# A second level of seven products for one unit of a fused attention and MLP kernel

## The chip, the cores and the metric

The kernel runs on one core of one Trainium2 chip. The metric is the device time of one execution in microseconds (us). The kernel before was run three times: median 203.09 us, from 202.88 to 203.41. Besides, one execution was taken with the hardware profiler; it took 203.15 us, and its trace spans 201.3 us from the first to the last instruction. TensorE had its full clock all the time.

## The reference

```
B, H, S, Ns, D = 8, 8, 512, 32, 64;  d_model, d_ff = 512, 2048
a     = softmax(x @ state^T / sqrt(D))            # per batch and head
xread = a @ state                                 # 512 rows of a batch
sread = softmax(state @ x^T / sqrt(D)) @ x        # 32 rows of a batch
h     = concat([xread, sread]) as (B * 544, 512)  # heads side by side
out   = gelu(h @ w_in) @ w_out                    # w_in 512 x 2048, w_out 2048 x 512
```

Inputs and output are fp32. The kernel computes its products in bf16 and sums them in fp32.

## The kernel before, in words

**Stages.** The eight batches b = 0 to 7 are done one after the other. For the 512 token rows of a batch, `state` and `w_in` are first multiplied (`p_mm`, L435), which gives P (256 x 2048, in two halves t); it is copied out of PSUM by ScalarE (ACT) and VectorE (DVE). The attention weights of a batch are made one batch ahead: `scores` (L325), `norm` (L347) on DVE, a transpose by DMA (`atr_dma`). A block `M` (`mm1`, L501) is two matmuls of 128x128 by 512 columns and a Gelu on ACT; 16 blocks make the hidden rows g of a batch (128 x 16 x 512).

**The second product by seven.** The product g @ w_out of batches 1 to 7 isn't done by eight quarter products but by seven, in the manner of Strassen and Winograd. The contraction (16 chunks of 128), the token rows (256 and 256) and the output columns (256 and 256) are each cut in two. A unit `X(b, name)` (L651) is one of these products: 16 matmuls of 128x128 by 256 columns. Units "1", "2" and "4" read quarters of g as they are; "5", "6", "7" and "3" read sums that `g_sum` (L608) makes on DVE. The differences of w_out for the right operand are made once by `w_diff` (L563). The units collect in four PSUM banks, o0 to o3: bank 0 has "2", bank 1 "1", "6" and "7", bank 2 "5" and "3", bank 3 "4" (`BANK`, L642). Between units of a bank, ACT takes a copy (`snap`, L647: c2, c4, u, s5), and DVE adds bank and copy into the output rows (`add`, L644), which SP sends out. Unit "2" of batch b fills c2; the addition behind unit "1" reads it.

**The read-outs.** The 32 state rows of a batch (sread) are a sum over the batch's tokens: `reads_mm` (L886) does 32 small matmuls per batch with the copy `xo` of x, ACT copies the bank (`sraw`), DVE divides (`reads_norm`, L903), and `srts` (L421) transposes the result into XSR. For all batches together they go through w_in and w_out in batch 7 (`read_out_slot`, `SR`, `R`). `rearr_ones` (L230) makes `xo` on GpSimd (POOL) from batch 2 on, `rearr` (L221) the copy `x4` for the transposes. Each has two buffers, for even and odd batches. `hold_for` (L942) makes the POOL queue wait for a block's Gelu, so that a load behind it is issued no earlier.

**What sets the order.** There is no scheduler: every engine runs its instructions in the order of the code, and waits only for what an instruction needs. For b = 2 to 7 the code goes through eight slot pairs p = 0 to 7, each with the blocks 2p and 2p+1 of the batch. Units "1", "6", "5" and "7" of the batch before follow in p = 0, 1, 2 and 3, unit "3" in p = 5. Also in p = 5, `p_all` (L917) does the reads of this batch and the whole P of the next, with ACT and DVE copies; its tiles take o0, o1, o3 and o2 and four buffers of a second pool with the tag f, which also holds the results of the blocks and the scores. Then come unit "2" (p = 5) and unit "4" (p = 7) of the batch itself. In batches 2 to 5 the read of the batch itself is done in p = 5, in batch 6 those of 6 and 7.

The lines of the profile that belong to these steps: L626 units, L506 blocks, L441 P, L931 its copies, L893 reads, L901 `sraw`, L424 and L429 transposes of the reads, L616 g sums, L645 additions, L649 snaps, L757 and L775 sums for the read-outs, L797 and L863 read-outs, L225 and L235 copies on POOL.

Of the kernel before, what the change touches and what calls it, by code (L numbers as in the profile page):

```python
# [9 lines left out]
FP32 = mybir.dt.float32  # L10
BF16 = mybir.dt.bfloat16
# [6 lines left out]
def kernel(  # L18
# [36 lines left out]
    def otile(shape, name, at=None):  # L55
        if at is None:
            at = turn[0] % 4
            turn[0] += 1
        return ps_o.tile(shape, FP32, name=name, tag=f"o{at}")
# [55 lines left out]
    def load_x(b):  # L115
        xb = xin.tile([128, H, SJ * D], BF16, name="xb", tag="xb")
        nc.gpsimd.dma_start(out=xb, in_=xr[b])
        xbs[b] = xb
# [111 lines left out]
    def rearr_ones(b):  # L230
        A = atts[b]
        eng = nc.vector if b < 2 else nc.gpsimd
        src = xbs[b].rearrange("p (t c) (j d) -> p t c j d", t=2, d=D)
        for t in range(2):
            eng.tensor_copy(  # L235
                out=A.xo[:, :, :, 2 + 64 * t:66 + 64 * t].rearrange("p j c d -> p c j d"),
                in_=src[:, t],
            )
# [222 lines left out]
    def burst(chunks, b_read=None):  # L461
        done = []
        first = len(chunks) < 4 and b_read is not None
        if first:
            sread(b_read)
        for i, (b, f) in enumerate(chunks):
            done.append((b, f, p_mm(b, f, ftile if i < 2 else otile)))
        for x in done[:2]:
            p_copy(*x)
        if b_read is not None and not first:  # L470
            sread(b_read)
        for x in done[2:3]:
            p_copy(*x)
        if b_read is not None:
            sread_out(b_read)
        for x in done[3:]:
            p_copy(*x)
# [66 lines left out]
    def mm2_m(b, m):  # L544
        for j in range(SJ):
            if m == 0:
                ops[b, j] = otile([128, d_model], "op")
            nc.tensor.matmul(  # L548
                ops[b, j],
                lhsT=gs[b][:, m, j * 128:(j + 1) * 128],  # L550
                rhs=w_out_bf[:, m, :],
                start=(m == 0),
                stop=(m == MC - 1),
            )
# [23 lines left out]
    def w_rhs(name):  # L578
        return {"1": b11, "2": b21, "3": b22}.get(name) if name in "123" else w_t[name]

    xs = {}
    left, right = slice(0, NH), slice(NH, d_model)
    G_SUMS = {
# [7 lines left out]
    def g_q(b, h, k):  # L591
        return gs[b][:, MH * k:MH * k + MH, 256 * h:256 * h + 256]
# [15 lines left out]
    def g_sum(b, names, home=None):  # L608
        got = g_lhs.setdefault(b, {})
        for name in names:  # L610
            x, y, op = chain(name, lambda h, k: g_q(b, h, k), got)
            if home is None:
                got[name] = apool.tile([128, MH, 256], BF16, name="gsum", tag="gsum")
            else:
                got[name] = home
            nc.vector.tensor_tensor(out=got[name], in0=x, in1=y, op=op)  # L616
# [18 lines left out]
    def c_tile(name):  # L635
        return cpool.tile([128, 2, NH], FP32, name=name, tag=name)
# [7 lines left out]
    def add(out, x, y):  # L644
        nc.vector.tensor_tensor(out=out, in0=x, in1=y, op=ALU.add)  # L645
# [37 lines left out]

    def c21(b):
        add(xs[b, "o", 1][:, :, left], xs[b, 1], xs[b, "c4"])

    def rows_out(h, js, ns, eng):
        b = B - 1
# [197 lines left out]
    def reads_mm(bs):  # L886
        sr = ftile([128, len(bs), 2, 65], "sr")
        for i, b in enumerate(bs):
            A = atts[b]
            for t in range(2):  # L890
                for j in range(SJ):
                    for c in range(HC):
                        nc.tensor.matmul(  # L893
                            sr[32 * c:32 * c + 32, i, t, :],
                            lhsT=A.e[:, 2 * j + t, 32 * c:32 * c + 32],
                            rhs=A.xo[:, j, c, 1 + 65 * t:66 + 65 * t],
                            start=(j == 0),
                            stop=(j == SJ - 1),
                        )
        raw = cpool.tile([128, len(bs), 130], FP32, name="sraw", tag="sraw")  # L900
        nc.scalar.copy(out=raw, in_=sr.rearrange("q i t d -> q i (t d)"))  # L901
        return raw

    def reads_norm(bs, raw):
        for i, b in enumerate(bs):
            A = atts[b]
            A.srm = att.tile([128, 2, D], BF16, name="srm", tag="srm")
            inv = att.tile([128, 2], FP32, name="inv", tag="inv")
            nc.vector.reciprocal(out=inv, in_=raw[:, i, 0:130:129])
            nc.vector.tensor_tensor(  # L910
                out=A.srm,
                in0=raw[:, i, 1:129].rearrange("q (t d) -> q t d", t=2),
                in1=inv[:, :].to_broadcast((128, 2, D)),
                op=ALU.mult,
            )

    def p_all(nb, bs):  # L917
        raw = reads_mm(bs)
        done = []
        for f, at in enumerate(((0, None), (None, None), (1, 3), (2, None))):  # L920
            it = iter(at)

            def tiles(shape, name):
                i = next(it)
                return ftile(shape, name) if i is None else otile(shape, name, i)

            done.append((nb, f, p_mm(nb, f, tiles)))
        for b, f, ps in done:
            for t in range(2):
                copy = nc.scalar.copy if t == 0 or f == 0 else nc.vector.tensor_copy  # L930
                copy(out=Ps[b][:, t, f * 512:(f + 1) * 512], in_=ps[t])  # L931
        reads_norm(bs, raw)

    def p_copy_s(b, f, ps):
        for t in range(2):
# [153 lines left out]
    atr(1)  # L1089
    mm2_m(0, 9)  # L1090
    burst([(1, 1), (0, 3)])
    mm2_m(0, 10)
    M(16, 17)
    M(12, 13)
# [51 lines left out]
    for b in range(2, B):  # L1146
        nb = b + 1
        for p in range(8):
            k = 16 * b + 2 * p
            if p == 1 and nb < B:  # L1150
                scores(nb, 0)
                scores(nb, 1)
            if p in (2, 3) and nb < B and (b > 2 or p == 2):
                norm(nb, p - 2)
            if p == 3 and nb + 1 < B:
                xtr_dma(nb + 1)
            if p == 5 and nb < B:
                atr_dma(nb)
            if nb == B and p < 5:
                read_out_slot(p)  # L1160
                if p == 4:
                    r_homes()
                    r_sum("56")
                continue
            if b != 2 or p != 3:
                M(k, k + 1)
            if b == 2 and p == 2:
                M(k + 2, k + 3)
            if b == 2 and p == 1:
                w_diff("7")  # L1170
            if p < 5 and nb < B:
                if p == 0:
                    g_sum(b - 1, "56")
                if p == 2:
                    g_sum(b - 1, "7")
                if p == 3:
                    g_sum(b - 1, "3")
                if p < 4:
                    X(b - 1, "1657"[p])
                if b == 2 and p == 2:  # L1180
                    norm(3, 1)
                    for x in [(2, f, p_mm(2, f, ftile)) for f in (2, 3)]:
                        p_copy(*x)
                if p == 1 and b > 2:
                    sr_w("5216"[b - 3])
            if p == 0 and b + 3 < B:
                hold_for(b, 0)
                load_x(4 if b == 2 else b + 3)
            if p == 6 and b == 2:
                hold_for(b, 12)  # L1190
                load_x(5)
            if p == 0 and nb + 1 < B:
                begin(nb + 1)
                rearr(nb + 1)
            if nb == B:
                if p == 5:
                    R("2")
                    r_sum("73")
                    R("4")
                if p == 6:  # L1200
                    R("1")
                    X(b, "2")
                    R("6")
                    R("5")
                if p == 7:
                    X(b, "4")
                continue
            if p == 5:
                X(b - 1, "3")
                reads = (b, nb) if nb == B - 1 else (b,)  # L1210
                p_all(nb, reads)
                if b == 2:
                    rearr_ones(3)
                    rearr_ones(4)
                elif nb + 1 < B:
                    rearr_ones(nb + 1)
                X(b, "2")
            if p == 7:
                srts(reads)
                X(b, "4")  # L1220
    b = B - 1
    g_sum(b, "56")
# [41 lines left out]
```

## Time and profile before

| | |
|---|---|
| runs | 202.88, 203.09, 203.41 us |
| the profiled execution | 203.15 us, its span 201.3 us |
| a batch (67.4 to 88.6, 88.6 to 109.8, 109.8 to 131.0) | 21.2 us |
| in 88.6 to 109.8: busy PE, DVE, ACT, POOL | 21.15, 15.88, 16.76, 5.30 us |
| one unit (L626), 16 matmuls | 1.75 us on the chain |
| one block pair (L506), 4 matmuls | 0.86 us on the chain |

PE is TensorE's matmuls, PEld its weight loads, DVE VectorE, ACT ScalarE, POOL GpSimd, SP SyncE, whose queue issues DMAs. A row of a group has line, engine, operation, output and inputs, shapes and count, then busy us and mean ns of one, then the idle time before them and who ended it. A row of a timeline has start, duration and the instructions merged in it. A row of the chain has start, duration and what the end of the program waited for then. Matmuls overlap: a row of 16 lasts 0.16 us longer than the next matmul waits.

### The profile page before, as it was taken

How to read it: one execution, taken by the hardware profiler on the slowest of the kernel's cores; microseconds unless marked ns; L12 is line 12 of the kernel's file. 1: busy time of each engine (PE TensorE's matmuls, PEld its weight loads, DVE VectorE, ACT ScalarE, POOL GpSimd, SP SyncE). 2: the span in 40 equal slices, each digit the busy share in tenths (PEclk: the TensorE clock that was granted, in tenths of full speed). 3: DMA queues.
4: the chain of work that ended last, by engine and by line, in shares of the span. 5: the costliest groups of instructions: out<-in, count | busy, mean ns of one | idle time of the engine just before them, and what ended most of it. 6: DMA issues, size and time to landing. Idle time of an engine off the chain costs nothing.

```text
span 201.3 us, 4865 instructions
## 1 busy us (share of the span) xinstructions
PE 195.5 (97%) x2035; PEld 134.6 (67%) x2035; DVE 140.9 (70%) x235; ACT 142.8 (71%) x260; POOL 49.8 (25%) x63
## 2 busy tenths in 40 slices
PE   7899999999999999999999999999999999999994
PEld 2533544465767677676776687677776888878893
DVE  2873774789988569856795678467936787960863
ACT  3684677699896789668967797598948678774220
POOL 8973404423409444040503400120000000000000
PEclk9999999999999999999999999999999999999999
DMA  6999999977594979670696024520128010040054
GB/s 192 188 173 199 206 199 201 188 133 139 90 147 78 227 89 158 133 210 2 71 193 203 9 70 91 147 65 16 37 103 109 3 52 3 4 155 0 7 154 156
DMA packets 40567, 23.16 MB, mean 115 GB/s; under 512 B 21857, under 2 KB 39137, under 8 KB 40545
## 3 DMA queue, kind: packets, MB, share of 16 engines
q0 software_dynamic: 13984, 8.10, 29.9%
q1 hardware_dynamic: 25728, 14.22, 29.3%
q10 hardware_dynamic: 832, 0.52, 0.8%
q8 instruction: 16, 0.26, 0.5%
q14 instruction: 7, 0.05, 0.1%
HBM read 17.30 MB, written 8.91 MB: 130 GB/s over the span
## 4 chain that ended last, share of the span: by engine, by line
PE 91%; DMA 3%; ACT 2%; DVE 1%; issue 1%; SPq 0%; ACTq 0%
PE xp L626 41%; PE hp L506 27%; PE op L548 5%; PE sp L797 3%; PE rp L863 3%; DMA x0f<-in_x_dram 3%; PE op L532 2%; PE xp L704 2%; PE p_ps L441 2%; PE pt L333 2%; ACT P L931 1%; PE sr L893 1%; PE hp L1041 1%; PE aT_ps L374 1%; ACT sraw L901 1%
## 5 line engine op out<-in xcount | busy, mean ns | idle before, releaser
L513 ACT ACTIVATE g<-hp 128x512 bf16<-128x512 f32 x124 | 65.9, 609 | 13.6 <-PE hp L506 13.4
L506 PE MATMUL hp<-AT,P 128*128 128x512 bf16 x248 | 61.0, 379 | 0.0
L626 PEld LDWEIGHTS <-gsum 128*128 128x128 bf16 x416 | 40.5, 98 | 9.4 <-issue 0.4
L626 PE MATMUL xp<-ws,gsum 128*128 128x256 bf16 x320 | 38.2, 273 | 0.0
L506 PEld LDWEIGHTS <-P 128*128 128x128 bf16 x248 | 23.4, 98 | 21.1 <-ACT P L452 0.7
L626 PEld LDWEIGHTS <-g 128*128 128x128 bf16 x336 | 32.5, 98 | 7.1 <-issue 1.6
L626 PE MATMUL xp<-w_out_bf,g 128*128 128x256 bf16 x224 | 26.7, 272 | 0.3
L235 POOL COPY xo<-xb 128x1024 bf16<-128x1024 bf16 x12 | 13.2, 1129 | 36.4 <-PE sr L893 36.4
L616 DVE TENSOR_TENSOR gsum<-g 128x2048 bf16<-128x2048 bf16 x14 | 17.1, 1221 | 5.1 <-ACT g L513 4.5
L225 POOL COPY x<-xb 128x1024 bf16<-128x1024 bf16 x12 | 12.5, 1069 | 18.2 <-DMA xb<-in_x_dram 18.2
L649 ACT COPY c<-xp 128x512 f32<-128x512 f32 x14 | 8.3, 593 | 8.9 <-ACT g L513 3.9
L645 DVE TENSOR_TENSOR oh<-xp,c 128x512 f32<-128x512 f32 x14 | 9.6, 686 | 6.7 <-PE xp L626 6.7
L626 PE MATMUL xp<-ws,g 128*128 128x256 bf16 x112 | 13.4, 273 | 0.0
L931 ACT CAST P<-p_ps 128x512 bf16<-128x512 f32 x25 | 12.7, 608 | 0.1
L645 DVE TENSOR_TENSOR oh<-xp,u 128x512 f32<-128x512 f32 (+2 forms) x9 | 5.2, 573 | 10.8 <-PE xp L626 10.4
L548 PE MATMUL op<-w_out_bf,g 128*128 128x512 bf16 x48 | 11.8, 380 | 0.0
L626 PE MATMUL xp<-w_out_bf,gsum 128*128 128x256 bf16 x96 | 11.5, 273 | 0.0
L356 DVE TENSOR_TENSOR a<-e,ics 128x512 bf16<-128x512 bf16 x14 | 10.5, 750 | 0.5
L931 DVE CAST P<-p_ps 128x512 bf16<-128x512 f32 x15 | 9.4, 685 | 1.7 <-PE p_ps L441 1.7
L353 DVE TENSOR_REDUCE cs<-e 128x16 f32<-128x512 bf16 x14 | 9.5, 679 | 0.9 <-ACT e L340 0.9
L429 DVE COPY XSR<-srT 128x128 bf16<-128x128 bf16 (+1 forms) x5 | 3.4, 671 | 8.7 <-PE srT L424 8.7
L513 ACT ACT_TABLE_LOAD x7 | 9.0, 1283 | 0.1
(138 smaller groups left out, 256.5 us busy)
## 6 DMA issues: line engine op xcount, KB each, us to landing
out_dram<-oh SPq DMA_DIRECT2D x15, 256.0 KB, 2.4
xb<-in_x_dram POOLq DMA_DIRECT2D x7, 512.0 KB, 7.0
out_dram<-oh SPq DMA_DIRECT2D x6, 512.0 KB, 2.9
w_in_bf<-in_moe_w_in_dram POOLq DMA_DIRECT2D x6, 256.0 KB, 11.8
out_dram<-osb SPq DMA_DIRECT2D x5, 256.0 KB, 3.0
w_out_bf<-in_moe_w_out_dram POOLq DMA_DIRECT2D x4, 256.0 KB, 8.4
w_out_bf<-in_moe_w_out_dram POOLq DMA_DIRECT2D x2, 512.0 KB, 13.3
x0f<-in_x_dram SPq DMA_DIRECT2D x3, 256.0 KB, 3.8
```

The source lines that it names most:

```text
L225: nc.gpsimd.tensor_copy(out=A.x4[:, :, :, 64 * t:64 * t + 64].rearrange("p j c d -> p c j d"), in_=src[:, t],)
L235: eng.tensor_copy(out=A.xo[:, :, :, 2 + 64 * t:66 + 64 * t].rearrange("p j c d -> p c j d"), in_=src[:, t],)
L353: nc.vector.reduce_sum(out=cs, in_=e4, axis=AX.X)
L356: nc.vector.tensor_tensor(out=A.a[:, :, hs].rearrange("p g (c n) -> p g c n", n=NS), in0=e4, in1=ics[:, :, :].to_broadcast((128, G, 2, NS) ...
L506: nc.tensor.matmul(hp, lhsT=Ps[b][:, t, m * 128:(m + 1) * 128], rhs=atts[b].AT[:, :, t, :], start=(t == 0), stop=(t == 1),)
L513: nc.scalar.activation(out=gs[b][:, m, :], in_=hp, func=AF.Gelu)
L548: nc.tensor.matmul(ops[b, j], lhsT=gs[b][:, m, j * 128:(j + 1) * 128], rhs=w_out_bf[:, m, :], start=(m == 0), stop=(m == MC - 1),)
L616: nc.vector.tensor_tensor(out=got[name], in0=x, in1=y, op=op)
L626: nc.tensor.matmul(ps[:, j - js[0], :], lhsT=lhs[:, m, 128 * j:128 * j + 128], rhs=rhs[:, m, :], start=(first and j == js[0] and m == 0), ...
L645: nc.vector.tensor_tensor(out=out, in0=x, in1=y, op=ALU.add)
L649: nc.scalar.copy(out=xs[b, name], in_=ps)
L931: copy(out=Ps[b][:, t, f * 512:(f + 1) * 512], in_=ps[t])
```

## The change

Unit "2" of batches 2 to 6 is itself computed by seven products of half its size in each direction: the contraction is cut into 4 and 4 chunks, the tokens into 128 and 128, the columns into 128 and 128. Each product is 4 matmuls of 128x128 by 128 columns, 28 in all. All are collected in the bank o0, in four places of 128 columns.

- `w_subs` makes four differences of a quarter of w_out on DVE, once, behind the burst of batch 1.
- `sub_sums(b)` makes four sums of g (128 x 512 each) on DVE in p = 3, behind unit "7" of the batch before.
- `sub_a(b)` stands where unit "2" stood: products "2", "1", "4", "5" (16 matmuls), then an ACT copy qa of the bank.
- `sub_b(b)` follows blocks 12 and 13 in p = 6: products "6" and "3" onto two of the places and "7" into the first (12 matmuls), an ACT copy qb, and three DVE additions that make c2.

Besides, in the same edit:

- The reads are done in pairs: batches 2 and 3 in batch 2, 4 and 5 in batch 4, 6 and 7 in batch 6 as before. Their transposes come in p = 2 of batches 3 and 5, those of 6 and 7 in p = 7 of batch 6. The copy `xo` of batch 3 moves from p = 5 to p = 1 of batch 2, behind a hold for block 2.
- In batches 3 and 5 block 11 comes behind unit "3" (the fifth unit of the slots), instead of before it.
- The ACT copies of the third and fourth P tile (t = 0) come behind the qa copy.

```diff
+    QN = NH // 2
+    q_w = persist.tile([128, 4, MH // 2, QN], BF16, name="q_w", tag="mix3")
...
+    def w_subs():
+        sub = ALU.subtract
+        for i, (x, y) in enumerate((
+            (w_sub(1, 1), w_sub(1, 0)),
+            (w_sub(0, 1), q_w[:, 0]),
+            (w_sub(0, 1), w_sub(1, 1)),
+            (w_sub(0, 0), q_w[:, 1]),
+        )):
+            nc.vector.tensor_tensor(out=q_w[:, i], in0=x, in1=y, op=sub)
...
+    def sub_sums(b):
+        t = apool.tile([128, 4, MH // 2, 128], BF16, name="gsub", tag="gsum")
+        got = xs[b, "sub"] = {}
+        for i, name in enumerate("5673"):
+            x, y, op = chain(name, sub_q(b), got)
+            got[name] = t[:, i]
+            nc.vector.tensor_tensor(out=t[:, i], in0=x, in1=y, op=op)
+
+    def sub_mm(b, name, at, start=False):
+        lhs = chain(name, sub_q(b), {})[0] if name in "124" else xs[b, "sub"][name]
+        rhs = sub_rhs(name)
+        for m in range(MH // 2):
+            nc.tensor.matmul(
+                xs[b, 0][:, at, :],
+                lhsT=lhs[:, m, :],
+                rhs=rhs[:, m, :],
+                start=(start and m == 0),
+                stop=(m == MH // 2 - 1),
+                skip_group_check=True,
+            )
+
+    def sub_a(b):
+        xs[b, 0] = otile([128, 4, QN], "xp", 0)
+        for at, name in enumerate("2145"):
+            sub_mm(b, name, at, at == 0)
+        xs[b, "qa"] = cpool.tile([128, 4, QN], FP32, name="qa", tag="s5")
+        nc.scalar.copy(out=xs[b, "qa"], in_=xs[b, 0])
+
+    def sub_b(b):
+        sub_mm(b, "6", 1)
+        sub_mm(b, "3", 3)
+        sub_mm(b, "7", 0, True)
+        qa = xs[b, "qa"]
+        qb = cpool.tile([128, 4, QN], FP32, name="qb", tag="u")
+        nc.scalar.copy(out=qb, in_=xs[b, 0])
+        c = xs[b, "c2"] = c_tile("c2")
+        c = c.rearrange("p j (n w) -> p j n w", n=2)
+        add(c[:, 0], qb[:, 1:2, :].broadcast_to([128, 2, QN]), qb[:, 0:4:3, :])
+        add(c[:, 1], c[:, 0, 0:1, :].broadcast_to([128, 2, QN]), qa[:, 2:4, :])
+        add(c[:, 0, 0, :], qa[:, 1, :], qa[:, 0, :])
...
     def p_all(nb, bs):
-        raw = reads_mm(bs)
+        raw = reads_mm(bs) if bs else None
...
             for t in range(2):
+                if f >= 2 and t == 0:
+                    continue
                 copy = nc.scalar.copy if t == 0 or f == 0 else nc.vector.tensor_copy
...
-        reads_norm(bs, raw)
+        if bs:
+            reads_norm(bs, raw)
+        return done[2:]
...
     burst([(1, 1), (0, 3)])
+    w_subs()
...
-            if b != 2 or p != 3:
+            late = p == 5 and b % 2 and nb < B
+            if late:
+                M(k)
+            elif b != 2 or p != 3:
                 M(k, k + 1)
...
                 if p == 2:
+                    if b % 2:
+                        srts((b - 1, b))
                     g_sum(b - 1, "7")
...
                 if p < 4:
                     X(b - 1, "1657"[p])
+                if p == 3:
+                    sub_sums(b)
...
+            if p == 1 and b == 2:
+                hold_for(b, 2)
+                rearr_ones(3)
...
             if p == 5:
                 X(b - 1, "3")
-                reads = (b, nb) if nb == B - 1 else (b,)
-                p_all(nb, reads)
+                if late:
+                    M(k + 1)
+                reads = (b, nb) if b % 2 == 0 else ()
+                rest = p_all(nb, reads)
                 if b == 2:
-                    rearr_ones(3)
                     rearr_ones(4)
                 elif nb + 1 < B:
                     rearr_ones(nb + 1)
-                X(b, "2")
+                sub_a(b)
+                for _, f, ps in rest:
+                    nc.scalar.copy(out=Ps[nb][:, 0, f * 512:(f + 1) * 512], in_=ps[0])
+            if p == 6:
+                sub_b(b)
             if p == 7:
-                srts(reads)
+                if nb == B - 1:
+                    srts(reads)
                 X(b, "4")
```

More of the change, by code (lines that the diff above doesn't have):

```diff
@@ L579, in w_rhs, with w_sub, sub_rhs @@
         return {"1": b11, "2": b21, "3": b22}.get(name) if name in "123" else w_t[name]
+    QN = NH // 2
+    q_w = persist.tile([128, 4, MH // 2, QN], BF16, name="q_w", tag="mix3")
+    def w_sub(k, n):
+        return b21[:, MH // 2 * k:MH // 2 * k + MH // 2, QN * n:QN * n + QN]
+    def w_subs():
[7 more added lines that the diff above has]
+            nc.vector.tensor_tensor(out=q_w[:, i], in0=x, in1=y, op=sub)
+    def sub_rhs(name):
+        if name in "123":
+            return {"1": w_sub(1, 0), "2": w_sub(0, 0), "3": w_sub(0, 1)}[name]
+        return q_w[:, "5674".index(name)]
     xs = {}
@@ L685, in c21, with sub_q, q @@
         add(xs[b, "o", 1][:, :, left], xs[b, 1], xs[b, "c4"])
+    def sub_q(b):
+        def q(h, k):
+            g = g_q(b, 0, 0)
+            return g[:, MH // 2 * k:MH // 2 * k + MH // 2, 128 * h:128 * h + 128]
+        return q
+    def sub_sums(b):
[35 more added lines that the diff above has]
+        add(c[:, 0, 0, :], qa[:, 1, :], qa[:, 0, :])
     def rows_out(h, js, ns, eng):
```

## The prediction, on record before the result

> **What bounds the kernel.** I read the page's busy table and chain first, then the chain in order of time, then the timeline of each engine where the chain leaves TensorE. All times are us; the profiled execution took 203.15 around a span of 201.3, the runs shown have the median 203.09, so sums made on the trace are lowered by 0.06.
>
> ```profile
> PE 195.5 (97%) x2035; PEld 134.6 (67%) x2035; DVE 140.9 (70%) x235; ACT 142.8 (71%) x260; POOL 49.8 (25%) x63
> ...
> PE 91%; DMA 3%; ACT 2%; DVE 1%; issue 1%; SPq 0%; ACTq 0%
> ```
>
> TensorE is the bound: 91% of the chain is its own, most of the rest is the start. A batch takes 21.2. What is won must be won in matmul time, and any other engine that makes TensorE wait takes it back at once. One place per batch leaves TensorE already, the fifth slot pair (batch 3 here):
>
> ```profile
> 87.18 0.43 PE sr L893 x28
> ...
> 87.69 0.27 ACT sraw L901
> 87.96 0.58 ACT P L931
> 88.53 0.04 issue
> 88.58 1.91 PE xp L626 x16
> 90.48 1.73 PE hp L506 x8
> ...
> 158.84 0.89 PE sp L797 x16
> ```
>
> Unit "2" (88.58) writes bank o0, which the first P tile also used, so it starts 0.04 after ACT has copied that tile. The last line has 16 matmuls of 128 columns: 0.89/16 = 0.0557 each.
>
> **The matmuls.** Removed per batch: 16 matmuls of 256 columns, 1.74 (starts 88.58 to 90.32, the next block). Added: 16 + 12 of 128 columns, 28 x 0.0557 = 1.56. Saved 0.18, five times: **-0.90**.
> The Trainium skill's "TensorE: Matmul & The Clock Gate", section "Back-to-back issue gap", speaks against the change: it puts a stream of weight loads and matmuls at some 81 ns each for 128 columns, by which the 28 would take 2.27 and each batch lose 0.53. The read-out rows of this trace, the same shape with a weight load for each, show 56 ns, so the row decides.
>
> **The wait at the fifth unit.** From the start of unit "3" to that of unit "2" one read takes 85.27 to 88.58 = 3.31, two reads (batch 6) 148.91 to 152.48 = 3.57. Batches 2 and 4 become pairs, +0.26 each; batch 6 stays one. Batches 3 and 5 have no read, but block 11 after unit "3": its two matmuls end 0.60 after the unit's last issue (0.22 + 0.38), the Gelu starts at 0.64, the next ACT work 0.485 later (four Gelus take 2.06, one 0.61), so the P copy runs 1.13 to 1.73 and the next unit starts at 1.78. With 1.75 for unit "3" that is 3.53, of which 0.43 stood in front of it: 3.10, so -0.21 each. TensorE alone would be through at 1.51 (block 0.43, change of tile shape 0.09, P matmuls 0.99). Sum: 2 x 0.26 - 2 x 0.21 = **+0.10**.
>
> **ACT behind it.** Let S be the start of the new unit. Its matmuls are issued until S+0.89, end at S+1.06; ACT has finished three P copies by S+0.92 and makes the qa copy S+1.14 to 1.72 (snap rows: 0.08 after the matmul, 0.58 long). Part two, behind blocks 12 and 13, comes at S+1.76, when the copy has just released the bank: 0, and 0.15 per batch if the cover fails. Then f2, f3, two Gelus, qb (S+3.6 to 4.15) and the last two Gelus, at 0.485 each, end at S+5.15; the next batch's unit "1" needs them at S+5.9. ACT's extra copy (0.59) is hidden.
>
> **DVE.** The costs of its sizes by the nearest rows:
>
> ```profile
> L616 DVE TENSOR_TENSOR gsum<-g 128x2048 bf16<-128x2048 bf16 x14 | 17.1, 1221 | 5.1 <-ACT g L513 4.5
> L841 DVE TENSOR_TENSOR rs<-g_sr 128x1024 bf16<-128x1024 bf16 x2 | 1.4, 683 | 0.0
> L775 DVE TENSOR_TENSOR srx<-XSR 128x256 bf16<-128x256 bf16 x5 | 1.2, 286 | 0.0
> ```
>
> A sum of 512 lies between the last two, 0.42 on a line through them; four, two of them waiting for the one before, 1.6. The three c2 additions have 256, 256 and 128 fp32 values, 0.43 + 0.43 + 0.29 (L645 rows of these sizes), S+4.2 to 5.3; g sums wait for the Gelu at S+5.15 anyway and end at S+7.8, before unit "6" at S+8.9. The sub-sums follow the c21 addition; in batches 4 to 6 DVE is idle there for 1.86 to 2.13: 0. The four weight differences after the burst at 31: DVE idles 1.62, 0.32 and 1.22 before 37.5, 0, or 0.3 if POOL's copies at 32.59 hold them. The joint XSR copy (0.43) stands before g sum "7" in batches 3 and 5, which ended 0.9 and 1.7 ahead of its unit: 0.
>
> **Moved steps.** The transposes of the reads (0.06 each on TensorE) go from the end of a batch to the third slot pair of the next, six before and after: 0. On POOL the new hold (0.19 where nothing blocks it, 48.57) and the two copies of batch 3 stand in the order that the trace has already, since the copies ran at 62.27, behind the others, before their slot pair 5 was reached. The Gelu of block 12 comes some 0.8 later, and with it the hold before the load of batch 5 (70.57) and its copies (76.94); SP's transpose of them (79.24) is needed one batch later. SP gets nothing new. No queue holds anybody by this, and I take 0 with an upper end of 0.2.
>
> **Batch 6 into the read-outs.** Here the pair's XSR copy follows the additions: DVE S+5.3 to 5.72, first read-out sum at 6.05. TensorE would be at the first read-out at 6.02 and starts at 6.1; g sums "5" and "6" run to 8.73, the addition after read-out "4" (L818, 0.69) to 9.34, so read-out "2", due at 9.19, starts at 9.39. The next block starts at S+9.84, before at S+9.73. Instead of -0.18, batch 6 gives +0.11: **+0.29**.
>
> **The port.** This decides the forecast. DVE sums from SBUF and POOL copies do not run side by side:
>
> ```profile
> 61.67 1.74 DVE L616 TENSOR_TENSOR gsum<-g,gsum 128x2048 bf16<-128x2048 bf16 x1
> ...
> 63.94 0.67 DVE L645 TENSOR_TENSOR oh<-xp,c 128x512 f32<-128x512 f32 x1
> 65.95 0.69 DVE L645 TENSOR_TENSOR oh<-xp,u 128x512 f32<-128x512 f32 x1 [1.34 <-PE xp L626]
> ```
>
> ```profile
> 62.27 3.03 POOL L235 COPY xo<-xb 128x1024 bf16<-128x1024 bf16 x2
> 66.23 2.03 POOL L235 COPY xo<-xb 128x1024 bf16<-128x1024 bf16 x2 [0.93 <-PE sr L893]
> ```
>
> The sum took 1.74 for 1.22 beside POOL, and POOL's pair 3.03 for 2.03 beside the sum; additions with one operand in PSUM keep their 0.68. At 97.27 two sums (0.68 each) took 2.61 while POOL's pair took its 2.02, so POOL can hold DVE for a whole copy.
> The Trainium skill's "SBUF — State Buffer", section "Who interferes with whom", agrees and adds that issue order decides who blocks.
>
> In batch 2, POOL's copies for batch 3 now stand behind a hold and start at 63.4 when the sum ends; the second runs 64.4 to 65.45. The sub-sums, free at 64.61, start there and need 1.5, to 66.95. At 66.23 the reads release POOL's copies for batch 4 into their middle. Behind the sub-sums DVE has the addition that frees bank o2 (0.69), and the P matmuls for o2 come at 67.12 (64.00 + 3.57 - 1.11 + 0.66). Nothing between: addition to 67.55, P at 67.6, S 0.35 later at 67.95, for 67.57: +0.4. One copy (1.05) between: **+1.4**, both +2.4. I take one copy, as each side can win a hand-over in the rows above.
>
> In batch 3, POOL's copy for batch 5, which waited 8.29 for the read until 87.50, is free since batch 2's pair and follows the other two at once (76.94 to 79.22, now some 0.8 later): four copies, until 81.8, beside the softmax product and g sum "7". That sum ended at 80.90; its unit is due at 82.3 then. If DVE wins a turn, 0.2 late, if not a copy more, 1.3; **+0.2**, the nearer to the 61.67 row. In batch 4 six copies run to 115.2, and the additions wait there, with g sums at 118.8 before unit "6" at 118.9: 0, or 0.5.
>
> **Sum.** -0.90 + 0.10 + 0.29 + 1.4 + 0.2 = +1.09, 203.15 to 204.24, on the scale of the median **204.2**. About 0.3%, 0.6, is what a measurement can tell from no change.
>
> **Rivals.**
> *DVE keeps the port in batch 2*: +0.4 for 1.4, sum +0.09, 203.2. For it: DVE's next sum is queued before the last one ends. Against: the two rows at 97.
> *All is covered, faster*: in batch 2 the sums end by 66.4, so the addition frees o2 by 67.12; that is the point from which it decides, and it needs the sums some 0.5 earlier, by being shorter than the line gives or by starting before POOL's second copy. Batch 3 loses nothing. Then -0.51, 202.6; if in batches 3 and 5 ACT also keeps up with TensorE (1.51 for 1.78), -0.54 more, 202.0; middle 202.4. For it: nearly every DVE idle time there is longer than the new work. Against: the release at 66.23 lies inside them.
> *POOL wins every turn*: 2.4 in batch 2, with 0.2 to 1.5 in batch 3: +2.1 to +3.4, 205.2 to 206.5, middle 205.8.
> *The change does not save*: 81 against 56 ns would show in the 28 matmuls; the rows exclude it.
>
> **Chances.** Forecast 0.40; DVE keeps the port 0.18; all covered 0.28, of which 0.22 below 202.5; POOL wins all 0.14. Faster 0.22, same 0.18 + 0.06 = 0.24, slower 0.54. The range 202.3 to 205.9 leaves out the far halves of the two outer cases; the 0.15 per batch and 0.3 and 0.5 lie inside. Forecast's own range 203.6 to 204.8.
>
> **What would show it.** Right: 128-column xp matmuls at 56 ns; 3.57 before the unit in batches 2, 4, 6 and about 3.53 in 3 and 5; in batch 2 a gsub sum of over 1 us, a late addition at L645, and a gap of TensorE before the P matmuls; POOL's copies for batch 5 right behind 79. Wrong: gsub sums of 0.4 in batch 2 (then 203.2 or less), or a wait of TensorE for qa at S+1.76, which would add to every batch.

## The result and the profile after

The changed kernel took 203.52 us (median of 11 runs, 203.03 to 204.17), the kernel before 202.84 in 11 runs beside it (202.36 to 203.41): a ratio of 1.0037, 95% interval 1.0026 to 1.0049. That is 0.68 us slower, in the direction forecast; the forecast's +1.1 was too much. The profiled execution took 203.52, with a span of 201.8.

The page of the changed kernel, its busy times and its chain by engine:

```profile
PE 194.6 (96%) x2095; PEld 134.1 (66%) x2095; DVE 156.5 (78%) x272; ACT 145.2 (72%) x263; POOL 51.5 (26%) x64
...
PE 82%; DVE 6%; DMA 4%; POOL 4%; ACT 2%; issue 1%; POOLq 0%; DVEq 0%
```

TensorE has 60 instructions more and 0.9 us less to do: that is the saving. DVE has 15.6 more, and its share of the chain went from 1% to 6%. Followed in order of time, the chain now runs through DVE in two places that TensorE held before but for one ACT copy, 31 to 36 (batch 1) and 61 to 68 (batch 2). In batch 3, the place that was shown of before, the chain is:

```profile
88.42 0.60 ACT g L513
89.02 0.48 ACT P L1002
89.50 0.04 issue
89.55 1.05 PE xp L727 x16
90.60 0.86 PE hp L506 x4
91.46 0.67 PE xp L727 x12
```

The unit's two parts (L727) are on the chain with 1.05 and 0.67 where one row of 1.91 stood. Nothing stands between part one, the blocks 12 and 13 and part two: the feared wait for qa is not there.

**Where the time went.** The two profiled executions start differently (the row named next comes at 33.77 before and at 33.29 after, ahead of anything that waits for the change), so I measure between starts of TensorE rows. The *first stretch* runs from the transpose of batch 1's read (`srT`, L416 in both kernels) to the start of unit "3" in batch 2, the *body* from there to the end of the last matmul. The last columns are the times from unit "3" to the first part of the new unit.

| kernel | first stretch | body | b 2 | b 3 | b 4 | b 5 | b 6 |
|---|---|---|---|---|---|---|---|
| before | 30.23 | 134.32 | 3.36 | 3.31 | 3.31 | 3.31 | 3.58 |
| changed | 30.83 | 134.62 | 4.56 | 3.50 | 3.61 | 3.50 | 3.57 |
| e1, differences later | 30.23 | 134.68 | 4.62 | 3.50 | 3.61 | 3.50 | 3.57 |
| e2, sums behind unit "3" | 30.87 | 135.81 | 3.67 | 3.50 | 3.61 | 3.50 | 3.57 |
| e3, two copies left out | 30.87 | 134.35 | 3.79 | 3.50 | 3.70 | 3.50 | 3.57 |
| e4, pairs alone | 30.23 | 134.45 | 3.67 | 3.50 | 3.61 | 3.50 | 3.57 |
| e5, copies moved | 30.47 | 133.79 | 3.68 | 3.50 | 3.61 | 3.50 | 3.62 |
| e6, e5 and late additions | 30.36 | 133.61 | 3.69 | 3.50 | 3.61 | 3.50 | 3.57 |
| e7, e5 and block 11 back | 31.22 | 133.75 | 3.69 | 3.03 | 3.61 | 3.03 | 3.63 |
| e8, single reads | 30.62 | 133.76 | 3.60 | 3.31 | 3.31 | 3.36 | 3.63 |
| e9, e6 and early copies | 30.23 | 133.66 | 3.74 | 3.50 | 3.61 | 3.50 | 3.62 |

Two losses stand out in the row of the changed kernel: +0.60 in the first stretch, and in batch 2 4.56 where the pair of reads alone (e4) gives 3.67. The body gained and lost: five units 5 x -0.18 = -0.90; reads and block 11 +0.13 (e4 against before: +0.31, +0.30 and twice 3.50 - 3.31 - 0.43); batch 2 +0.89 (4.56 against e4's 3.67); batch 6 +0.18 (e6). Together +0.30, which is what the body shows.

**The place in batch 2**, the timeline of DVE in the changed kernel (start, duration):

```profile
64.54 1.17 DVE L721 TENSOR_TENSOR gsub<-g 128x512 bf16<-128x512 bf16 x1
65.75 0.42 DVE L721 TENSOR_TENSOR gsub<-gsub,g 128x512 bf16<-128x512 bf16 x1
66.09 0.42 DVE L721 TENSOR_TENSOR gsub<-g 128x512 bf16<-128x512 bf16 x1
66.42 1.26 DVE L721 TENSOR_TENSOR gsub<-g,gsub 128x512 bf16<-128x512 bf16 x1
67.61 0.68 DVE L666 TENSOR_TENSOR oh<-xp,u 128x512 f32<-128x512 f32 x1
```

POOL of the changed kernel beside it:

```profile
63.41 2.03 POOL L235 COPY xo<-xb 128x1024 bf16<-128x1024 bf16 x2
66.36 2.24 POOL L235 COPY xo<-xb 128x1024 bf16<-128x1024 bf16 x2 [0.92 <-PE sr L962]
```

And TensorE:

```profile
68.34 0.41 PE L441 MATMUL p_ps<-w_in_bf,sbd 64*32 64x512 bf16 x8 [0.88 <-DVE oh L666]
68.68 0.62 PE L727 MATMUL xp<-w_out_bf,g 128*128 128x128 bf16 x8
```

Two of the four sums took 0.42, two took 1.17 and 1.26: the first beside POOL's second copy for batch 3 (until 65.44), the last beside the first copy for batch 4, which the reads released at 66.36. The addition behind the sums, which frees bank o2, came at 67.61, and TensorE waited 0.88 for it with its last eight P matmuls. This is the mechanism of the forecast, its copy included.

**The place in batch 1**, which the forecast had at nothing, in the changed kernel's chain:

```profile
31.88 0.34 DVE q_w L595
32.25 1.36 DVE q_w L595 x2
...
33.77 1.25 DVE q_w L595
35.02 0.65 DVE XSR L419
35.67 0.04 issue
35.71 1.02 PE hp L506 x4
```

POOL's row of that time:

```profile
32.38 2.37 POOL L225 COPY x<-xb 128x1024 bf16<-128x1024 bf16 x2 [7.58 <-DMA xb<-in_x_dram]
```

The four differences (`w_subs`, L595) ran from 31.80 to 35.02, 3.22 where e1 will show 1.76 with only the first of them beside the end of POOL's copies, since two of them took turns with POOL's two copies. Behind them in DVE's queue stands the small copy of `srT` into XSR (L419). Nobody needs XSR for a long time, but `srT` lies in a buffer with the tag f, and the next block needs that buffer. TensorE:

```profile
35.71 1.02 PE L506 MATMUL hp<-AT,P 128*128 128x512 bf16 x4 [0.44 <-DVE XSR L419]
```

### The profile page after: what moved, and what is told of

It reads as the page before. It is cut to its first block, busy times and chain, and to the rows that moved or that the text cites. A ratio compares the mean times of both kernels' runs of the same rounds, so it can differ in the third digit from the quotient of the medians.

```text
span 201.8 us, 5024 instructions
## 1 busy us (share of the span) xinstructions
PE 194.6 (96%) x2095; PEld 134.1 (66%) x2095; DVE 156.5 (78%) x272; ACT 145.2 (72%) x263; POOL 51.5 (26%) x64
## 4 chain that ended last, share of the span: by engine, by line
PE 82%; DVE 6%; DMA 4%; POOL 4%; ACT 2%; issue 1%; POOLq 0%; DVEq 0%
PE xp L647 35%; PE hp L506 25%; PE xp L727 4%; DMA w_in_bf<-in_moe_w_in_dram 4%; PE sp L866 3%; PE op L548 3%; PE rp L932 3%; PE op L532 2%; PE xp L773 2%; POOL w_in_bf L105 2%; PE pt L333 2%; PE p_ps L441 2%; DVE gsub L721 2%; DVE q_w L595 1%; DVE P L453 1%; DVE oh L666 1%
## 5 line engine op out<-in xcount | busy, mean ns | idle before, releaser
L513 ACT ACTIVATE g<-hp 128x512 bf16<-128x512 f32 x124 | 67.0, 612 | 17.4 <-PE hp L506 17.2
L506 PE MATMUL hp<-AT,P 128*128 128x512 bf16 x248 | 62.1, 379 | 0.4 <-DVE XSR L419 0.4
L647 PEld LDWEIGHTS <-g 128*128 128x128 bf16 x256 | 24.9, 98 | 4.9
L637 DVE TENSOR_TENSOR gsum<-g 128x2048 bf16<-128x2048 bf16 x14 | 17.6, 1255 | 4.6 <-ACT g L513 4.5
L647 PE MATMUL xp<-w_out_bf,g 128*128 128x256 bf16 x144 | 17.2, 273 | 0.0
L235 POOL COPY xo<-xb 128x1024 bf16<-128x1024 bf16 x12 | 14.0, 1196 | 11.0 <-PE sr L962 11.0
L666 DVE TENSOR_TENSOR oh<-xp,c 128x512 f32<-128x512 f32 x14 | 9.6, 685 | 2.3 <-PE xp L647 2.0
L441 PE MATMUL p_ps<-w_in_bf,sbd 64*32 64x512 bf16 x248 | 9.7, 381 | 1.2 <-DVE oh L666 0.9
L666 DVE TENSOR_TENSOR c<-qb 128x256 f32<-128x256 f32 x5 | 2.5, 506 | 9.7 <-ACT qb L749 9.7
L1016 POOL COPY hold<-g 128x1 bf16<-128x1 bf16 x6 | 3.2, 527 | 24.8 <-ACT g L513 24.8
L637 DVE TENSOR_TENSOR gsum<-gsum,g 128x2048 bf16<-128x2048 bf16 x7 | 8.6, 1225 | 0.2
```

Of the source, the lines that this page charges most:

```text
L235: eng.tensor_copy(out=A.xo[:, :, :, 2 + 64 * t:66 + 64 * t].rearrange("p j c d -> p c j d"), in_=src[:, t],)
L441: nc.tensor.matmul(ps[t][32 * c:32 * c + 32, :], lhsT=sbd[64 * t:64 * t + 64, b, c, 32 * t:32 * t + 32], rhs=w_in_bf[64 * t:64 * t + 64, c ...
L506: nc.tensor.matmul(hp, lhsT=Ps[b][:, t, m * 128:(m + 1) * 128], rhs=atts[b].AT[:, :, t, :], start=(t == 0), stop=(t == 1),)
L513: nc.scalar.activation(out=gs[b][:, m, :], in_=hp, func=AF.Gelu)
L647: nc.tensor.matmul(ps[:, j - js[0], :], lhsT=lhs[:, m, 128 * j:128 * j + 128], rhs=rhs[:, m, :], start=(first and j == js[0] and m == 0), ...
```

## The experiments

The theory: the change does save 0.18 per unit, and what it costs are two places where DVE's new sums meet POOL's copies, batch 1 (+0.60) and batch 2 (+0.89), with small change from the pairs of reads and batch 6. Rivals: that the pairs or the moved block cost more than they seem to, that the second level itself disturbs, and that the waits come from the order of DVE's queue whoever holds the port. Each ratio is against the kernel before, run beside it (median 202.81 for e1 to e4, 202.59 for e5 to e8, 202.95 for e9).

### e1: the weight differences later

```diff
     burst([(1, 1), (0, 3)])
-    w_subs()
     mm2_m(0, 10)
     M(16, 17)
     M(12, 13)
     srt(1)
+    w_subs()
     M(14, 15)
```

> The four weight differences come behind the copy of the read's transpose (XSR of batch 1) on DVE instead of ahead of it; nothing else moves. Theory: ahead of that copy they hold it until 35.66, its PSUM buffer with the tag f with it, and blocks 16/18 of the start wait 0.60 for that buffer. Then the time falls by about 0.6 against the changed kernel, to some 0.0 to +0.1 us against the kernel before, and the block pair after the srT follows its predecessor with no DVE release. Rival: DVE's 1.5 to 3 us of work beside POOL's copies is what costs, and comes back at the next evictions (L519): less than 0.2 us faster than the changed kernel.

Measured: 202.93 (12 runs), ratio 1.0004 (0.9985 to 1.0023), which can't be told from before any more. DVE's timeline in this run:

```profile
33.39 0.73 DVE L419 COPY XSR<-srT 128x128 bf16<-128x128 bf16 x1 [1.62 <-PE srT L416]
33.75 0.63 DVE L595 TENSOR_TENSOR q_w<-w_out_bf 128x512 bf16<-128x512 bf16 x1
```

The copy runs at once, the differences behind it take 0.63, 0.42, 0.42 and 0.42, and the first stretch is back at 30.23. The same four instructions cost 0.60 in one place and nothing one step later: it was their place ahead of the copy, beside POOL.

### e2: the sums of batch 2 behind unit "3"

```diff
                 if p < 4:
                     X(b - 1, "1657"[p])
-                if p == 3:
+                if p == 3 and b != 2:
                     sub_sums(b)
...
             if p == 5:
                 X(b - 1, "3")
+                if b == 2:
+                    sub_sums(b)
```

> In batch 2 alone the four sub-sums come behind the addition after unit 3 on DVE, not ahead of it. Theory: of the sub-sums' delay by POOL's copies only the addition behind them costs, since it frees bank o2 for the P matmuls; then unit 3 to the new unit in batch 2 takes 3.6 us instead of 4.56, the time falls by 0.9 us against the changed kernel. Rival: the sub-sums themselves, pushed later into POOL's copies for batch 4, are then late for product 5, or the P copies behind them are late for blocks 14 and 15: the gap moves behind the start of the unit, and less than 0.4 is won.

Measured: 204.34 (8 runs), ratio 1.0066 (1.0040 to 1.0092). The 0.9 expected was not won: the ratio is above the changed kernel's 1.0037, though the intervals overlap, and the body is 1.19 longer in the traces. The wait for o2 is gone (3.67 instead of 4.56), but other waits came in its place, as the rival said. Two stand out. TensorE of this run:

```profile
70.48 0.59 PE L506 MATMUL hp<-AT,P 128*128 128x512 bf16 x2 [0.90 <-DVE P L1002]
...
84.48 0.72 PE L647 MATMUL xp<-ws,gsum 128*128 128x256 bf16 x5 [0.54 <-DVE gsum L637]
```

The sums now ended at 69.83, still with two of them at 1.00 and 1.14 beside POOL, and the P copies of DVE stood behind them, so block 13 waited 0.90 for a buffer. So it is not this addition that matters but everything behind the sums in DVE's queue, as long as POOL's copies lie beside them. The second wait is the one forecast for batch 3. DVE of this run there:

```profile
77.61 2.92 DVE L826 TENSOR_TENSOR srw<-w_in_bf 128x1024 bf16<-128x1024 bf16 x2
...
83.21 1.21 DVE L637 TENSOR_TENSOR gsum<-g 128x2048 bf16<-128x2048 bf16 x1
```

Four copies of POOL in a row (77.50 to 82.41) made the two sums take 2.92 for 1.4 and the product 1.51 for 0.69; g sum "7" ended at 84.42, and unit "7" started 1.02 behind its due time. In the changed kernel the read-out sums came 0.46 earlier and POOL's copies 0.84 later, so the sums escaped (1.28). The copies held the softmax product (1.55) and the g sum itself instead:

```profile
81.16 1.72 DVE L637 TENSOR_TENSOR gsum<-g 128x2048 bf16<-128x2048 bf16 x1
```

It ended at 82.88, and unit "7" was just on time (83.00). Whether batch 3 loses 0 or 1.0 is decided by shifts of less than 1 us upstream.

### e3: POOL's two copies for batch 4 left out

```diff
                 if b == 2:
-                    rearr_ones(4)
+                    pass
                 elif nb + 1 < B:
```

This kernel leaves out the copy `xo` of batch 4, so the reads of batch 4 use old data.

> POOL's two copies of x for the reads of batch 4 are left out (the reads of batch 4 use old data); everything else is the changed kernel. Theory: the fourth sub-sum then takes 0.42 instead of 1.27, the sums end at about 66.9, the addition at 67.5, and the new unit of batch 2 starts 4.0 us after unit 3, 0.55 to 0.7 sooner than in the changed kernel; the first sub-sum still waits for the copies for batch 3. Rival: bank o2 or the sums are not what the P matmuls wait for: unit 3 to the new unit stays at 4.5 us and the time within 0.2 of the changed kernel's.

Measured: 203.29 (12 runs), ratio 1.0017 (1.0000 to 1.0035). DVE's last sum in batch 2, 1.26 in the changed kernel, and the addition behind it:

```profile
66.99 0.42 DVE L721 TENSOR_TENSOR gsub<-g,gsub 128x512 bf16<-128x512 bf16 x1
67.32 0.68 DVE L666 TENSOR_TENSOR oh<-xp,u 128x512 f32<-128x512 f32 x1
```

Without the copies the last sum takes 0.42, and the new unit comes 3.79 behind unit "3", 0.77 sooner: most of the 0.89 hangs on these two copies, the rest (3.79 to 3.67) on the first sum's wait for the copy for batch 3, which is still 1.17 here. The body is only 0.27 shorter, since it loses 0.40 and 0.09 in batch 4: there POOL's copies for batch 6 held two read-out sums, and g sum "7" ended 0.34 behind the due time of its unit.

### e4: the pairs and the moved block alone

```diff
     burst([(1, 1), (0, 3)])
-    w_subs()
...
-                if p == 3:
-                    sub_sums(b)
...
-                sub_a(b)
                 for _, f, ps in rest:
                     nc.scalar.copy(out=Ps[nb][:, 0, f * 512:(f + 1) * 512], in_=ps[0])
-            if p == 6:
-                sub_b(b)
+                X(b, "2")
```

> Only the second half of the change: reads in pairs, block 11 behind unit 3, copies moved; unit 2 is one product of 16 matmuls as before, and there are no sub-sums and weight differences. Theory: 0.26 to 0.31 lost in batches 2 and 4 and 0.21 to 0.23 won in 3 and 5, no wait for o2: within 0.2 us of the kernel before, some +0.1. Rival: the pairs bring the loss (POOL's earlier copies for batch 5 hold DVE in batch 3, and the addition for o2 is late without the sums too): +0.6 us or more against the kernel before.

Measured: 202.58 (12 runs), ratio 0.9999 (0.9981 to 1.0016), body +0.13. The pairs, the moved block and the deferred P copies have the small price that the reads were given (+0.10), and the first stretch is that of before. The rival that they carry the loss falls.

### e5: POOL's copies out of the way

e1, and the copies for batch 3 at the load of batch 4, those for the next batches behind a hold that waits for a P copy (even batches) or block 11 (odd):

```diff
                 load_x(4 if b == 2 else b + 3)
-            if p == 1 and b == 2:
-                hold_for(b, 2)
-                rearr_ones(3)
+                if b == 2:
+                    rearr_ones(3)
...
                 rest = p_all(nb, reads)
-                if b == 2:
-                    rearr_ones(4)
-                elif nb + 1 < B:
+                if b % 2 == 0:
+                    nc.gpsimd.tensor_copy(out=hold, in_=Ps[nb][:, 0, 0:1])
+                else:
+                    hold_for(b, 11)
+                if nb + 1 < B:
                     rearr_ones(nb + 1)
                 sub_a(b)
```

> The weight differences come behind the XSR copy of batch 1 as in the run before, and POOL's copies are taken out of DVE's sums: those for the reads of batch 3 come ahead of the other copies of slot 0 of batch 2, those for 4 and 6 wait for the first P copy of ACT (the start of the new unit), those for 5 and 7 for the Gelu of block 11. Theory: sub-sums of 0.42 in every batch, unit 3 to the new unit 3.6 in batch 2 (4.6 before), no wait of unit 7 for its sum; from unit 3 of batch 2 to the last matmul some 133.7 us, 0.9 less than in the changed kernel, and about 0.8 us faster than the kernel before. Rival: DVE is so full that another of its sums is late, or POOL's copies at their new places hold the additions of c2 and the g sums: less than 0.4 won against the changed kernel's 134.6.

Measured: 202.81 (12 runs), ratio 1.0003 (0.9983 to 1.0023). DVE's last sum in batch 2 and the addition behind it, in this run:

```profile
65.66 0.42 DVE L721 TENSOR_TENSOR gsub<-g,gsub 128x512 bf16<-128x512 bf16 x1
66.00 0.69 DVE L666 TENSOR_TENSOR oh<-xp,u 128x512 f32<-128x512 f32 x1
```

The four sums take 0.41 to 0.42, the new unit comes after 3.68, and the body falls to 133.79, 0.53 below before: the second level's saving is there once the port is free. The time did not follow: 0.8 was expected. The first stretch was 0.24 longer than before, which is half of it, and the interval of 0.4 to either side can't tell the rest.

### e6: the additions of batch 6 behind the read's transposes

e5, with the three additions of c2 split off as `sub_c`:

```diff
             if p == 6:
                 sub_b(b)
+                if nb < B - 1:
+                    sub_c(b)
             if p == 7:
                 if nb == B - 1:
                     srts(reads)
+                    sub_c(b)
                 X(b, "4")
```

> The same, and in batch 6 the three additions that make c2 stand behind the XSR copy of the read-outs on DVE, not ahead of it. Theory: the wait of the first read-outs of 0.2 us (two units of 0.98 for 0.89 on the chain) is gone and the run is 0.2 faster than the one with the ports alone. Rival: the addition after read-out 4 still stands behind the g sums, and nothing changes.

Measured: 202.35 (12 runs), ratio 0.9988 (0.9975 to 1.0000). The chain at the read-outs of batch 6, first in the changed kernel:

```profile
159.08 0.98 PE sp L866 x16
...
161.81 0.98 PE sp L866 x16
```

and in this one:

```profile
157.70 0.89 PE sp L870 x16
...
160.34 0.89 PE sp L870 x16
```

Two read-outs of 0.98 became 0.89 again and the body is 0.18 shorter. So the additions ahead of the XSR copy did delay the read-outs, as forecast, by 0.18 instead of 0.29.

### e7: block 11 back in its place

e5, with one line changed:

```diff
-            late = p == 5 and b % 2 and nb < B
+            late = False
```

> The ports run with block 11 ahead of unit 3 again in batches 3 and 5. Theory: without its Gelu in front, ACT has copied the first P tile at 1.2 after the last matmul of unit 3 is issued, but the addition that frees o2 holds the last P matmuls to 0.97 and the new unit to 1.32: unit 3 to the new unit 3.1 with 0.43 more in front of it, so the same time within 0.1. Rival: block 11 is needed behind unit 3 to fill the wait, and its move back costs 0.3 or more in each of the two batches.

Measured: 202.72 (12 runs), ratio 1.0015 (0.9997 to 1.0033). The body is 133.75 for e5's 133.79: 3.03 before the new unit plus the 0.43 of the block in front of it is 3.46, against 3.50. Moving the block alone is worth nothing that shows. The first stretch is 0.99 longer than before, which the moved block, in batches 3 and 5, has no part in. 0.35 of it was lost ahead of the first unit, where TensorE waited for the transpose of x by DMA (42.19), the other 0.64 just ahead of unit "3" of batch 2. DVE of this run:

```profile
54.04 2.89 DVE L576 TENSOR_TENSOR ws<-w_out_bf 128x2048 bf16<-128x2048 bf16 x1
```

POOL beside it:

```profile
53.82 2.03 POOL L235 COPY xo<-xb 128x1024 bf16<-128x1024 bf16 x2
```

A difference of w_out that takes 1.22 alone waited out both copies for batch 3, in the place that e5 had given them. In e5, e6 and e8, which share it, the same difference took 3.06. DVE was late from then on: a softmax product (0.69 alone) fell beside POOL's next copies and took 0.94, 0.83 and 1.08 there and 1.50 here, and a block waited for the P copies behind it. Ahead of unit "3" that cost 0.24, 0.13, 0.39 and here 0.64, so e5's place for these copies was bad too.

### e8: single reads

e6 with one read per batch, its transposes in p = 7 and block 11 in front, as in the kernel before. POOL's hold waits for the P copy in every batch:

```diff
-            late = p == 5 and b % 2 and nb < B
+            late = False
...
                 if p == 2:
-                    if b % 2:
-                        srts((b - 1, b))
                     g_sum(b - 1, "7")
...
-                reads = (b, nb) if b % 2 == 0 else ()
+                reads = (b, nb) if nb == B - 1 else (b,)
                 rest = p_all(nb, reads)
-                if b % 2 == 0:
-                    nc.gpsimd.tensor_copy(out=hold, in_=Ps[nb][:, 0, 0:1])
-                else:
-                    hold_for(b, 11)
+                nc.gpsimd.tensor_copy(out=hold, in_=Ps[nb][:, 0, 0:1])
...
             if p == 7:
+                srts(reads)
                 if nb == B - 1:
-                    srts(reads)
+                    sub_c(b)
                 X(b, "4")
```

> The tail run with the reads of one batch each as in the kernel before (batch 6 with two), the transposes in slot 7 and block 11 ahead of unit 3: the second level of products without the pairs. Theory: unit 3 to the new unit 3.3 in batches 2 to 5 and 3.57 in 6; the pairs alone cost 0.1, so the same as the tail run or 0.1 to 0.2 faster. Rival: the pairs are needed to make the second level pay, since a read in every batch keeps ACT and the f buffers busy when qa is due: part two waits, 0.5 or more slower than the tail run.

Measured: 202.27 (12 runs), ratio 0.9988 (0.9971 to 1.0005). The new unit comes 3.31 behind unit "3" in batches 3 and 4, just as before, and the body is 133.76 for e6's 133.61. The second level does not need the pairs: in the bodies of these two traces they are worth 0.15, which the runs do not show.

### e9: the early copies

e6, with the copies for batch 3 still earlier, where POOL is idle and DVE has no sums:

```diff
     load_st(3, B)
+    rearr_ones(3)
     M(18, 19)
...
                 load_x(4 if b == 2 else b + 3)
-                if b == 2:
-                    rearr_ones(3)
```

> The tail run with POOL's copies for the reads of batch 3 moved once more, from the first slot of batch 2 (where 0.1 to 1.0 us was lost between 34 and 64) to POOL's idle stretch at 42.6, behind the load of the later states. Theory: from the transpose of batch 1's read to unit 3 of batch 2 30.2 us as in the kernel before, from there to the last matmul 133.6; in all 0.7 us faster than the kernel before, and the runs closer together. Rival: there they hold the softmax products of batch 2 (44.6 and 46.3), the transpose of them by DMA is late for the first block of batch 2 at 50.7, and the first stretch stays at 30.5 or more: at most 0.4 faster.

Measured: 202.27 (7 runs, 201.46 to 202.78) against 202.95 (12 runs), ratio 0.9955 (0.9933 to 0.9977): 0.9 us (0.5 to 1.4) faster than before by the ratio, and with the changed kernel at 1.0037 it beats both. Batch 2 on DVE:

```profile
64.25 0.41 DVE L721 TENSOR_TENSOR gsub<-g 128x512 bf16<-128x512 bf16 x1
...
65.71 0.68 DVE L666 TENSOR_TENSOR oh<-xp,u 128x512 f32<-128x512 f32 x1
```

The four sums and the start of the addition fit into 1.46. First stretch 30.23, body 133.66: together 0.66 below before. The runs were expected closer together and are not (1.32 from lowest to highest, 1.14 before). That is the change as it was meant, with the new sums and POOL's copies kept apart almost everywhere (a g sum at 61.31 still took 1.82, at no cost). The copies were not moved in the kernel before alone. Its trace leaves little for that to win: unit "3" to unit "2" takes 3.36 in batch 2, where POOL's copies for batch 3 stand, and 3.31 in batches 3 to 5.

**How far the trace carries.** Stretch and body together, less those of before, against the ratio of the runs: changed +0.90 (runs +0.5 to +1.0), e1 +0.36 (-0.3 to +0.5), e3 +0.67 (0 to +0.7), e4 +0.13 (-0.4 to +0.3), e5 -0.29 (-0.3 to +0.5), e7 +0.42 (-0.1 to +0.7), e8 -0.17 (-0.6 to +0.1), e9 -0.66 (-1.4 to -0.5) agree. e2, +2.13 (+0.8 to +1.9), and e6, -0.58 (-0.5 to 0), lie just outside: one profiled execution stands for many there, and whichever side wins a hand-over can differ between executions.

## Why the prediction was right, and where it was not

- **The matmuls: right.** Saved 0.18 per unit, 16 matmuls of 128 columns in 0.89 as in the read-outs. That is 56 ns each; 81 ns is excluded, and with it the rival that the change does not save.
- **The fifth unit: right.** 3.61 in batch 4 for 3.57, 3.50 in batches 3 and 5 for 3.53; +0.13 for +0.10. Its cause for batches 3 and 5, ACT's Gelu and then its P copy, is in the chain. Moving block 11 is not needed for it: in e7, with the block in front, the time is the same.
- **ACT: right.** Part two follows blocks 12 and 13 without a wait in every batch; the cover of 0.15 per batch held.
- **Batch 2, the step that decided: right in mechanism, too large.** +0.89 for 1.4, the value for one copy of POOL between the sums; e3 and e5 show that it is the copies. The sums were done at 67.68, at 67.56 on the scale of before, where the working gives 68.0 (66.95 and a copy of 1.05). The sums that waited ended some 0.3 after POOL's copy, less than the 0.42 that one takes alone. "DVE keeps the port" (0.4) and "POOL wins every turn" (2.4) did not happen. "All is covered" needed o2 free by 67.12; the addition ended at 68.2 on that scale.
- **Batch 3: 0 for 0.2** in this execution, with the mechanism there: POOL's copies held g sum "7", which ended 0.12 ahead of its unit, and e2 shows 1.02 for it, inside the bounds given.
- **Batch 6: 0.18 for 0.29**, by the XSR copy behind the additions, as e6 shows.
- **Where it failed: "The four weight differences after the burst at 31: DVE idles 1.62, 0.32 and 1.22 before 37.5, 0, or 0.3 if POOL's copies at 32.59 hold them."** They cost 0.60, and e1 takes all of it back by moving them. The step saw the copies and summed DVE's idle time, but did not ask what is queued behind the differences: the XSR copy, whose PSUM buffer a block waits for. DVE of the kernel before:

```profile
34.02 0.73 DVE L419 COPY XSR<-srT 128x128 bf16<-128x128 bf16 x1 [1.62 <-PE srT L416]
```

  This 1.62 of idle time ahead of that copy was all the room there was, not 3.16, and the differences took 3.22.
- **The sum.** In its order the terms measure -0.90, +0.13, +0.18, +0.89 and 0, and +0.60 for the differences: +0.90, as the traces show from the transpose of batch 1 on; the runs say +0.68 (0.5 to 1.0). The total came as close as it did by luck, because errors of opposite sign cancel: 0.60 missed in batch 1, 0.51 too much in batch 2 and 0.3 in batches 3 and 6.

## What to carry to other kernels

When work is moved to an engine with idle time, sum that idle time only up to the next instruction in its queue that someone waits for, and count a copy that merely frees a rotating PSUM buffer as such an instruction. Sums from SBUF on VectorE and copies on GpSimd must be counted as one resource, as the rows of 1.17 to 1.26 for 0.42 show: give each its own stretch of time, and the saving is kept (e9, 0.45% faster than before) instead of eaten up (0.37% slower). Where two such queues meet, a shift of less than 1 us upstream decides whether a wait appears further down, so a fix has to be followed through the whole trace (e2, e3).

## What was not expected of the hardware

- **Hand-overs of the shared port.** Mostly the two sides alternate: in the changed kernel at 32 the third difference took 1.26 and the fourth 1.25 with one POOL copy for each. But a difference of w_out waited out two copies in a row in e7 (2.89 for 1.22 at 54.04), and in e5, e6 and e8 (3.06). What decides it stays open; no run was made for it.
- **A copy of one element per partition waits too.** POOL's hold, 128x1, takes 0.19 alone; beside a g sum of DVE it took 1.19 in the changed kernel (62.28). A hold meant to order a queue can be late by most of a sum.
- **Additions with an operand in PSUM do not take part**: those of 128x512 (`oh<-xp`, L666) kept 0.67 to 0.69 beside POOL's copies in every run. An addition of c2 on the same line, with both operands in SBUF, did: 0.83 for 0.43 beside a copy (114.98 in the changed kernel).
